# Attention and routed experts on one core: how the two halves of a head's output are added

## The chip, the cores and the metric

The kernel runs on one core of one Trainium2 chip. The metric is the device time of one execution in microseconds (us). A core has TensorE (PE in the profile; its weight loads are listed apart as PEld), VectorE (DVE), ScalarE (ACT), GpSimd (POOL), SyncE (SP, which issues most DMAs) and 16 DMA engines. Each engine takes its instructions in order and waits on semaphores for the others. SBUF is the on-chip memory of 128 partitions; PSUM holds what TensorE writes.

## What is computed

```python
# per batch b (4), head (8): q, k, v are 576 x 64
scores = 0.125 * rotate(q) @ rotate(k).T
attn = softmax(scores)                  # rows of 576
head = attn @ v                         # 576 x 64
x = heads side by side                  # 2304 tokens x 512
logits = x @ w_gate                     # 8 experts
gate = sigmoid(x @ w_local)             # keep the expert of the token before, or take a new one
out = p[e] * (relu(x @ w1[e]) @ w2[e])  # one expert e per token
```

All is float32, and the products are made precise enough for the choice of the expert: operands are split into a high and a low part (type fp32r), and the parts are multiplied apart.

## The kernel before

Two heads of one batch make a pair; there are 16 pairs. The attention goes in 144 steps, nine to a pair: a step g issues the scores of tile g+1 (`mm_s`, L267), the row minimum of it on VectorE (L272), the exponentials of tile g on ScalarE (L289), the transposes of tile g-2 (`tr_main`, L325, L335, L341) whose result is split by ScalarE (high part, L303) and VectorE (low part, L307), and up to five products of attention and values for a pair begun eleven steps ago (`pv_mm`, L361). Eight of the nine steps have five such products, one has none.

The pair's output is made in four units u, each of one half h of the tokens (288 columns) and one head a. The weights of the product are the high and the low part of v side by side (64 + 64 columns), so the 128 x 288 result in PSUM has the share of the high part in 64 partitions and that of the low part in the other 64, and these have to be added. `pv_evac` (L363 to L372) does it: ScalarE copies one half to SBUF at the other half's partitions (`tmp`, 64 x 288, L371), and VectorE adds it to the half that stays in PSUM (`xt`, 64 x 288, L372). The two heads of a pair stand in the two halves of one tile `xt` (128 x 576).

Some steps later `gates` (L417 to L460) turns the pair's output into rows of tokens: for each of five blocks of 128 tokens (the last overlaps the fourth) one float32 product with `xt` as the weights and the constant `wid` as the moving operand (L436, tile `gx`). `wid` is an identity of 128 columns with the 18 columns of the pair's gate weights beside it, so one product of 146 columns gives the rows of both heads and their gate scores. `rows(0, 3)` issues three blocks in the step that has no attention product, `rows(3, 2)` two in the next. VectorE scales the results (L444, L446), and DMAs write the rows to DRAM. A float32 product is two instructions on TensorE, each with a weight load of its own.

The order on TensorE is the order of the program (`MAN0`, `MAN2`). On VectorE, ScalarE, GpSimd and SyncE a scheduler of the framework sets the order from step 12 on, from the dependences and estimates of its own, so a change of one instruction there can move others. In the last part of the attention (about 246 to 302 us) the routing of three batches to the experts (`route`) is woven in, mostly on VectorE; then the experts' products follow (L940, L983) until the end, with the routing of the last batch at their begin.

PSUM tiles of one bank come from `ps_t` (four buffers: transposes, `pv`, `gx`), the score tiles from `ps_s` (two buffers of two banks).

Of the kernel before, what the change touches and what calls it, by code (L numbers as in the profile page):

```python
# [10 lines left out]
F32 = mybir.dt.float32  # L11
F32R = mybir.dt.float32r
BF16 = mybir.dt.bfloat16
# [4 lines left out]
ALU = mybir.AluOpType  # L18
AX = mybir.AxisListType

B, H, S, D = 4, 8, 576, 64
NE, DM, DF = 8, 512, 1024
NP = H // 2
NT = B * S
P = 128
NB = 5
NBLK = B * NB
NG = (B - 1) * NB
# [16 lines left out]
MANUAL = KE  # L45
QK_LAST = 121
SPREAD_LAST = 127

TILE_EARLY = ("ffAffsfxBssgCsshD", "ffAffxfsBsCsgsshD", "fffAffxBssChsgssD", "ffAfffxBsssshsCDg", "ffAfffBsssxsshCgD", "fffxAffsBssgssChD")
TILE = "ffHAgfffxBTssshsCsDL"  # L50
# [5 lines left out]
BIG = 4096.0  # L56
TWO23 = 2.0 ** 23
DX = DM + 1
GATES_AT = {13: 4, 14: 7, 15: 4}

SPLITS = (((1, 2, 3, 4, 5, 7), (0, 6)), ((0, 1, 3, 5, 6, 7), (5, 6)), ((3, 4, 5, 6), (1, 5, 6)), ((1, 3, 4, 7), (1, 3, 4)), ((0, 2, 4, 5, 6), (5, 6)), ((3,), (0, 7)), ((2, 5, 6, 7), (4,)))
# [1 line left out]
ZTHR = -1.5 * 2.0 ** -23  # L63

_COLS = {}
_off = 0
for _n, _w in (
    ("iota128", 128), ("code8", 8), ("p1", 1),
    ("keys", NBLK * NE), ("s0", NBLK), ("pad", NBLK), ("tok64", NBLK),
    ("scan0", 8 * NG + 8), ("tile128", 25),  # L70
):
    _COLS[_n] = (_off, _off + _w)
    _off += _w
# [3 lines left out]
def _constants():  # L77
    c = np.zeros((P, NCONST), np.float32)
    p = np.arange(P)

    def put(name, a):
        lo, hi = _COLS[name]
        if a.dtype == np.int32:
            c.view(np.int32)[:, lo:hi] = a
        else:
            c[:, lo:hi] = a

    put("iota128", np.arange(128)[None])
    put("code8", 7 - np.arange(8)[None])
    put("p1", p[:, None] + 1)  # L90
    tok = np.zeros((P, NBLK))
    tok64 = np.zeros((P, NBLK))
    s0 = np.zeros((P, NBLK))
    pad = np.zeros((P, NBLK))
    s0[0, ::NB] = 1
    pad[:64, 4::NB] = 64
    for b in range(B):
        for j in range(NB):
            lo = b * S + (j * 128 if j < 4 else S - 128)
            tok[:, b * NB + j] = lo + p  # L100
            tok64[:, b * NB + j] = lo // 64
    put("keys", (TWO23 + 8 * tok[:, :, None] + 7 - np.arange(8)).reshape(P, -1))
    put("s0", s0)
    put("pad", pad.astype(np.int32))
    put("tok64", tok64)
    sc = np.ones((8, NG + 1))
    sc[:, 0] = 0
    put("scan0", sc.reshape(1, -1))
    put("tile128", 128 * np.arange(25)[None])
    return c  # L110
# [27 lines left out]
def tile_attention_moe(ctx, tc, qk, v, tabs, turn, consts, tri, wg, wts, out):  # L138
    nc = tc.nc
    pe, act, dve, pool, sp = nc.tensor, nc.scalar, nc.vector, nc.gpsimd, nc.sync  # L140
    outf = out.rearrange("b s d -> (b s) d")

    const = ctx.enter_context(tc.tile_pool(name="const", bufs=1))
    pt_p = ctx.enter_context(tc.tile_pool(name="pt", bufs=4))
    pk_p = ctx.enter_context(tc.tile_pool(name="pk", bufs=4))
    xt_p = ctx.enter_context(tc.tile_pool(name="xt", bufs=XT))
# [7 lines left out]
    ps_t = ctx.enter_context(tc.tile_pool(name="ps_t", bufs=4, space=bass.MemoryType.PSUM))  # L154

    cst = const.tile([P, NCONST], F32, name="cst")
    C = {n: cst[:, a:b] for n, (a, b) in _COLS.items()}
    trib = const.tile([P, P], BF16, name="trib")
    onesb = const.tile([P, P], BF16, name="onesb")

    wid = const.tile([P, 2, 164], F32, name="wid")
    ident = wid[:, 0, 18:146]
    stage = const.tile([P, 7168], F32, name="stage")

    over = ctx.enter_context(tc.tile_pool(name="over", bufs=1))
# [12 lines left out]
    trif = stage[:, 7040:7168]  # L178

    v2_t, m_t, pthi, ptlo, pkhi, pklo, xt_t, sum_t = {}, {}, {}, {}, {}, {}, {}, {}  # L180
    s_t, e_t, tmp_t, pv_t = {}, {}, {}, {}
    qtail0 = None

    NPAIR = B * NP
# [178 lines left out]
    def pv_evac(p, u):  # L363
        h, a = divmod(u, 2)
        if u == 0:
            xt_t[p] = xt_p.tile([P, S], F32, tag="xt", name=f"xt_{p}")
            tmp_t[p] = xt_p.tile([P, S], F32, tag="xt", name=f"tmp_{p}")
        own, other = slice(64 * a, 64 * a + 64), slice(64 - 64 * a, 128 - 64 * a)
        hs = slice(h * HALF, (h + 1) * HALF)
        ps, tmp, xt = pv_t.pop((p, u)), tmp_t[p], xt_t[p]  # L370
        act.copy(tmp[own, hs], ps[other])  # L371
        dve.tensor_tensor(xt[own, hs], ps[own], tmp[own, hs], op=ALU.add)  # L372

    ohr = const.tile([P, NBLK, P], BF16, name="ohr")
    oha = const.tile([P, NBLK, NE], F32, name="oha")
# [41 lines left out]
    def gates(p):  # L417

        b, hp = divmod(p, NP)
        heads = slice(2 * hp, 2 * hp + 2)  # L420
        if hp == 0:
            gm_t[b] = small([P, NB, H, 9], "gm")
        r = sum_t[b].rearrange("p (h j) -> p h j", j=NB)[:, heads]

        def sums():
            act.copy(r[64:128, 1, 4:5], r[64:128, 0, 4:5])
            act.copy(r[64:128, 0, 4:5], r[0:64, 0, 4:5])
            flat = sum_t[b][:, 2 * hp * NB:(2 * hp + 2) * NB]
            act.add(flat, flat, 1e-9)
            dve.reciprocal(flat, flat)  # L430

        def rows(j0, n):
            ps = ps_t.tile([P, n, 146], F32, tag="t", name=f"gx_{p}_{j0}")
            for j in range(j0, j0 + n):
                lo = j * P if j < 4 else S - P
                pe.matmul(ps[:, j - j0], xt_t[p][:, lo:lo + P], wid[:, hp // 2, 18 * (hp % 2):18 * (hp % 2) + 146],  # L436
                          start=True, stop=True)
            rj = r[:, :, j0:j0 + n].rearrange("p a j -> p j a")
            xr = et_p.tile([P, S], F32, tag="et", name=f"xrow_{p}_{j0}")[:, 0:n * P]
            x = xr.rearrange("p (j a d) -> p j a d", a=2, d=D)  # L440
            o, w = ((18, 0), (0, 128))[hp % 2]
            px = ps[:, :, o:o + P].rearrange("p j (a d) -> p j a d", d=D)
            pw = ps[:, :, w:w + 18].rearrange("p j (a e) -> p j a e", e=9)
            dve.tensor_tensor(gm_t[b][:, j0:j0 + n, heads], pw, bc(rj, 3, 9), op=ALU.mult)  # L444
            if j0 == 0 or not ACT_ROWS:
                dve.tensor_tensor(x, px, bc(rj, 3, D), op=ALU.mult)  # L446
            else:
                for j in range(n):
                    for a in range(2):
                        act.activation(x[:, j, a], px[:, j, a], AF.Copy, scale=rj[:, j, a:a + 1])  # L450
            t0 = 1 + b * S
            cols = slice(P * hp, P * hp + P)
            m = min(j0 + n, 4) - j0
            sp.dma_start(rows_d[t0 + j0 * P:t0 + (j0 + m) * P, cols].rearrange("(j p) d -> p j d", p=P),
                         xr.rearrange("p (j d) -> p j d", d=P)[:, 0:m])
            if m < n:

                sp.dma_start(rows_d[t0 + 4 * P:t0 + S, cols], xr[64:128, m * P:n * P])

        return [sums, lambda: rows(0, 3), lambda: rows(3, 2)]  # L460
# [358 lines left out]
    other = []  # L819
# [84 lines left out]
    def gather(t):  # L904
# [6 lines left out]
        else:  # L911
# [3 lines left out]
        pool.indirect_dma_start(  # L915
            out=x[:, 0:DX], out_offset=None, in_=rows_d[0:top + 1],
            in_offset=bass.IndirectOffsetOnAxis(ap=gidx[:, t:t + 1], axis=0),
# [264 lines left out]
    if True:  # L1182
# [40 lines left out]
        for g in range(NSTEP):  # L1223
            if g == GM:
                begin.close()
            with tc.manual_schedule(engines=None if g < GM else MAN0):
                p, i = divmod(g, 9)
                if i == 0 and p % NP == 0:
                    b = p // NP
# [13 lines left out]

                if i == 0 and 2 <= p and p + 2 < NPAIR or g == SPREAD_LAST:
                    spread(p + 1)
# [24 lines left out]
                f = todo.pop(0) if todo else None  # L1270
# [55 lines left out]
def _laid_out(q, k, v, moe_w_gate, moe_w_local, moe_w1, moe_w2):  # L1326
    def turned(x):
        t = x.reshape(B, NP, 2, S, 2, D // 2).transpose(0, 1, 2, 4, 5, 3)
        x = np.stack([t.reshape(B, NP, 2, D, S), t[:, :, :, ::-1].reshape(B, NP, 2, D, S)], axis=4)
        x[:, :, 1] = x[:, :, 1, :, ::-1].copy()  # L1330

        for hp in range(2):
            y = x[0, hp].copy()
            y[1] = x[0, hp, 1, :, ::-1]
            x[0, hp] = y.transpose(2, 1, 0, 3)
        return x.reshape(B, NP, P, 2, S)

    qk = np.concatenate([turned(q), turned(k)], axis=3)
    vp = v.reshape(B, NP, 2, S, D)
    vm = vp[:, :, :, :512].reshape(B, NP, 8, P, D)  # L1340
    vt = np.zeros((B, NP, 2, P, D), np.float32)
    for a in range(2):
        vt[:, :, a, 64 * a:64 * a + 64] = vp[:, :, a, 512:]
    vv = np.concatenate([vm, vt], axis=2).transpose(0, 1, 3, 2, 4)
    w9 = np.concatenate([moe_w_gate, moe_w_local], axis=1).reshape(NP, 2, D, 9)
    wg = np.zeros((2, D, NP, 2, 9), np.float32)
    for a in range(2):
        wg[a, :, :, a] = w9[:, a].transpose(1, 0, 2)
    wg = wg.reshape(P, 2, 2, 18)
    eye = np.broadcast_to(np.eye(P, dtype=np.float32)[:, None], (P, 2, P))  # L1350
    wid = np.concatenate([wg[:, :, 0], eye, wg[:, :, 1]], axis=2)
    w1 = moe_w1.reshape(NE, 4, P, DF).transpose(0, 2, 1, 3).reshape(NE, P, 4 * DF)
    w2 = moe_w2.reshape(NE, 8, P, DM).transpose(0, 2, 1, 3).reshape(NE, P, 8 * DM)
    return {
        "qk": qk, "v": vv, "tabs": _tables(), "turn": _turn(), "consts": _constants(), "tri": _triangle(),
        "wg": wid, "wts": np.concatenate([w1, w2], axis=2),
    }
# [21 lines left out]
```

## Time and profile before

| | us |
|---|---|
| median of 3 runs | 542.3 (542.2 to 542.64) |
| profiled execution | 542.01 |
| its span (first to last instruction) | 540.2 |
| TensorE busy | 517.6 (96%) |
| VectorE busy | 387.3 (72%) |
| ScalarE busy | 345.3 (64%) |
| GpSimd busy | 330.1 (61%) |

The busy shares are means over two unlike parts. In the attention (up to about 302 us) TensorE, VectorE and ScalarE are all busy nearly throughout; in the experts' part TensorE alone is. The busy time of TensorE counts a matmul from its start to a modelled end, and successive ones overlap; the start of one weight load to the start of the next shows better what an instruction costs there. A line of the profile names source line, engine, operation, tiles (out<-in) and shapes.

### The profile page before, as it was taken

The numbers are of one execution on the slowest core, as the hardware profiler recorded it, in microseconds if no ns is written. First come the engines' busy times: TensorE is split into PE (matmuls) and PEld (weight loads), VectorE is DVE, ScalarE is ACT, GpSimd is POOL, SyncE is SP. The second block draws the span as 40 slices with busy tenths as digits, with TensorE's granted clock in tenths as the row PEclk, the third lists the DMA queues.
The fourth block names the chain that finished last, engine by engine and source line by source line (L and its number), as shares of the span: only waits on it lengthen the run. The fifth ranks groups of instructions, "written<-read, shape, count | busy, mean of one in ns | idle before, by whom it ended". The sixth has DMA issues, their size and how long they took to land.

```text
span 540.2 us, 10711 instructions
## 1 busy us (share of the span) xinstructions
PE 517.6 (96%) x3273; PEld 459.2 (85%) x3273; DVE 387.3 (72%) x725; ACT 345.3 (64%) x767; POOL 330.1 (61%) x245
## 2 busy tenths in 40 slices
PE   7989999999999999998999999999999999999993
PEld 4888999999999999997888788887888888888882
DVE  6998999999999999999999935528422736421731
ACT  4988889888999999987676623353533443532440
POOL 4998999888777988986598402337511455411332
PEclk9999999999999999999999999999999999999997
DMA  8659687866887787895288305371637495637350
GB/s 281 273 130 225 199 245 223 205 182 188 226 233 178 214 223 199 206 233 141 38 190 244 85 20 177 123 268 44 231 99 244 125 342 146 217 100 234 82 175 26
DMA packets 63610, 97.37 MB, mean 180 GB/s; under 512 B 28145, under 2 KB 38897, under 8 KB 61746
## 3 DMA queue, kind: packets, MB, share of 16 engines
q1 hardware_dynamic: 60066, 86.48, 56.3%
q0 software_dynamic: 3040, 9.71, 5.6%
q8 instruction: 28, 0.46, 0.3%
q14 instruction: 44, 0.36, 0.2%
q10 hardware_dynamic: 432, 0.36, 0.2%
HBM read 76.98 MB, written 12.86 MB: 166 GB/s over the span
## 4 chain that ended last, share of the span: by engine, by line
PE 63%; DVE 19%; ACT 8%; issue 5%; DMA 2%; POOL 2%; SPq 1%; POOLq 0%; DVEq 0%; ACTq 0%
PE h L940 18%; PE o L983 17%; PE s L267 8%; PE pv L361 8%; DVE mn L272 6%; PE tm L325 6%; DVE ptl L307 4%; ACT e L289 3%; ACT pth L303 2%; PE th L974 2%; PE tx L926 1%; DVE xt L372 1%; DVE pkl L307 1%; PE gx L436 1%; DVE w L885 1%
## 5 line engine op out<-in xcount | busy, mean ns | idle before, releaser
L983 PE MATMUL o<-w,hs 128*128 128x512 f32 x456 | 113.0, 397 | 0.0
L272 DVE TENSOR_REDUCE mn<-s 128x1 f32<-128x576 f32 x144 | 107.4, 746 | 4.1 <-PE s L267 2.7
L940 PE MATMUL h<-w,xs 128*128 128x512 f32 x444 | 106.1, 392 | 0.9 <-DVE xs L307 0.5
L289 ACT ACTIVATE e<-s,mn 128x576 f32<-128x576 f32 x128 | 95.2, 744 | 16.9 <-DVE mn L272 13.6
L267 PE MATMUL s<-m,qst 128*128 128x288 f32 x512 | 97.1, 310 | 6.1 <-ACT e L289 4.0
L307 DVE TENSOR_TENSOR ptl<-tm,pth 128x512 fp32r<-128x512 f32 x139 | 95.0, 684 | 6.5 <-ACT pth L303 3.4
L989 POOL DMA_INDIRECT out_dram<-os,sidx x19 | 23.3, 1227 | 124.0 <-ACTq L891 70.7
L940 PEld LDWEIGHTS h<-w,xs 128*128 128x128 f32 x444 | 82.5, 188 | 19.1 <-DVE w L885 1.1
L983 PEld LDWEIGHTS o<-w,hs 128*128 128x128 f32 x456 | 83.0, 188 | 17.0 <-DVE hs L307 0.4
L303 ACT CAST pth<-tm 128x512 fp32r<-128x512 f32 x139 | 80.9, 582 | 12.4 <-PE tm L325 11.3
L267 PEld LDWEIGHTS s<-m,qst 128*128 128x128 f32 x512 | 74.6, 188 | 12.0 <-ACT e L289 6.6
L325 PE MATMUL tm<-wid,e 128*128 128x128 f32 x512 | 77.0, 272 | 0.9 <-ACT e L289 0.5
L361 PE MATMUL pv<-pth,v 128*128 128x288 f32 x256 | 76.5, 314 | 0.4 <-DVE ptl L307 0.2
L361 PE MATMUL pv<-ptl,v 128*128 128x288 f32 x256 | 76.5, 314 | 0.0
L196 POOL TENSOR_TENSOR stage<-stage 128x1152 f32<-128x1152 f32 x26 | 69.0, 2665 | 8.1 <-DMA stage<-in_qk_dram 6.2
L325 PEld LDWEIGHTS tm<-wid,e 128*128 128x128 f32 x512 | 62.0, 140 | 1.7 <-ACT e L289 0.7
L885 DVE TENSOR_TENSOR w<-stage,w 128x1024 fp32r<-128x1024 f32 x37 | 50.9, 1409 | 15.3 <-DMA stage<-in_wts_dram 7.5
L361 PEld LDWEIGHTS pv<-pth,v 128*128 128x128 f32 x256 | 48.2, 188 | 2.9 <-DVE ptl L307 0.9
L361 PEld LDWEIGHTS pv<-ptl,v 128*128 128x128 f32 x256 | 48.3, 189 | 0.0
L307 DVE TENSOR_TENSOR xs<-tx,xs 128x512 fp32r<-128x512 f32 x19 | 13.1, 689 | 44.0 <-ACTq L891 34.3
L307 DVE TENSOR_TENSOR hs<-th,hs 128x512 fp32r<-128x512 f32 x26 | 17.5, 687 | 30.8 <-ACTq L891 19.1
L197 POOL TENSOR_TENSOR stage<-stage 128x576 f32<-128x576 f32 x26 | 37.0, 1430 | 0.2
(199 smaller groups left out, 814.1 us busy)
## 6 DMA issues: line engine op xcount, KB each, us to landing
stage<-in_wts_dram SPq DMA_DIRECT2D x84, 512.0 KB
stage<-in_qk_dram SPq DMA_DIRECT2D x13, 1152.0 KB
qst<-xq SPq DMA_DIRECT2D x56, 128.0 KB
stage<-in_v_dram SPq DMA_DIRECT2D x16, 320.0 KB
m<-xq SPq DMA_DIRECT2D x14, 288.0 KB
m<-xk SPq DMA_DIRECT2D x14, 288.0 KB
m<-xq SPq DMA_DIRECT2D x14, 256.0 KB
m<-xk SPq DMA_DIRECT2D x14, 256.0 KB
```

The costliest lines, as they stand in the source:

```text
L196: engine.tensor_tensor(x, x, tab[:, 2 * f:2 * f + 2], op=ALU.mult)
L197: engine.tensor_tensor(rr[:, f], x[:, 0], x[:, 1], op=ALU.add)
L267: pe.matmul(st[:, h, lo:hi], lhs, keys[:, k0:k0 + hi - lo], start=(n == 0), stop=(n == len(parts_) - 1))
L272: dve.tensor_reduce(mn, s_t[g][:, :, 0:HALF], axis=AX.XY, op=ALU.min)
L289: act.activation(dst.rearrange("p (h s) -> p h s", h=2), s_t.pop(g)[:, :, 0:HALF], AF.Exp, bias=mn, scale=-1.0, accum_out=sums[:, col:col ...
L303: act.copy(hi, src)
L307: dve.tensor_tensor(lo, src, hi.bitcast(F32), op=ALU.subtract)
L325: pe.transpose(ps[:, k], src[:, k * P:(k + 1) * P], ident)
L361: pe.matmul(pv_t[p, u], lhs.rearrange("p c d -> p (c d)"), rhs, start=(n == 0), stop=(n == 9))
L885: (pool if k in on_pool else dve).tensor_tensor(lo, src, hi.bitcast(F32), op=ALU.subtract)
L940: pe.matmul(ps[:, c], xs_t[t][:, x, k], w[y][:, c * 512:(c + 1) * 512], start=(k == 0 and n == 0), stop=(k == 3 and n == 2))
L983: pe.matmul(ps, hs_t[t][:, x, k], w[y][:, (k % 2) * 512:(k % 2 + 1) * 512], start=(k == 0 and n == 0), stop=(k == 7 and n == 2))
```

## The change

`pv_evac` has no addition any more: ScalarE copies all 128 partitions of the unit's result at once, and the two heads go to two tiles `xt0` and `xt1` (128 x 576 each, in the buffers that `xt` and `tmp` had). The sum is left to the product that turns the rows. For each block of tokens there are now two products, one for each head, each with that head's tile as the weights (128 partitions: high and low share) and 73 columns of the new `wid` as the moving operand: two 64 x 64 identities on top of each other, which add the shares, and beside them, also twice, the head's 9 gate columns. The result in PSUM has 146 columns a block, as before. `wid` grows from 328 to 456 columns; to make room, two constants (`iota128`, `scan0`) are kept in 16 bits, in half the columns, so that `consts` shrinks from 510 to 382 columns. `EVAC_DVE` lists units that VectorE would copy in place of ScalarE; it is empty.

```diff
+EVAC_DVE = ()
+WG = D + 18
+HALVES = ("iota128", "scan0")
...
-    wid = const.tile([P, 2, 164], F32, name="wid")
-    ident = wid[:, 0, 18:146]
+    wid = const.tile([P, P + NP * WG], F32, name="wid")
+    ident = wid[:, 0:P]
...
     def pv_evac(p, u):
         h, a = divmod(u, 2)
         if u == 0:
-            xt_t[p] = xt_p.tile([P, S], F32, tag="xt", name=f"xt_{p}")
-            tmp_t[p] = xt_p.tile([P, S], F32, tag="xt", name=f"tmp_{p}")
-        own, other = slice(64 * a, 64 * a + 64), slice(64 - 64 * a, 128 - 64 * a)
+            xt_t[p] = [xt_p.tile([P, S], F32, tag="xt", name=f"xt{a}_{p}") for a in range(2)]
         hs = slice(h * HALF, (h + 1) * HALF)
-        ps, tmp, xt = pv_t.pop((p, u)), tmp_t[p], xt_t[p]
-        act.copy(tmp[own, hs], ps[other])
-        dve.tensor_tensor(xt[own, hs], ps[own], tmp[own, hs], op=ALU.add)
+        ps, xt = pv_t.pop((p, u)), xt_t[p][a]
+        if u in EVAC_DVE:
+            dve.tensor_copy(xt[:, hs], ps)
+        else:
+            act.copy(xt[:, hs], ps)
...
-            ps = ps_t.tile([P, n, 146], F32, tag="t", name=f"gx_{p}_{j0}")
+            ps = ps_t.tile([P, n, 2 * WG], F32, tag="t", name=f"gx_{p}_{j0}")
             for j in range(j0, j0 + n):
                 lo = j * P if j < 4 else S - P
-                pe.matmul(ps[:, j - j0], xt_t[p][:, lo:lo + P], wid[:, hp // 2, 18 * (hp % 2):18 * (hp % 2) + 146],
-                          start=True, stop=True)
+                for a in range(2):
+                    w0 = P + hp * WG + (9 if a == 0 else 0)
+                    pe.matmul(ps[:, j - j0, a * (D + 9):(a + 1) * (D + 9)], xt_t[p][a][:, lo:lo + P], wid[:, w0:w0 + D + 9],
+                              start=True, stop=True)
...
-            o, w = ((18, 0), (0, 128))[hp % 2]
-            px = ps[:, :, o:o + P].rearrange("p j (a d) -> p j a d", d=D)
-            pw = ps[:, :, w:w + 18].rearrange("p j (a e) -> p j a e", e=9)
+            px = ps.rearrange("p j (a d) -> p j a d", a=2)[:, :, :, 0:D]
+            pw = ps[:, :, D:WG].rearrange("p j (a e) -> p j a e", e=9)
```

On TensorE the products that turn the rows become twice as many, at the same places. The program of the kernel before, with the products of pair 2 (`gx`) in the step of pair 5 that has no attention product, and the two blocks of the next step:

```order
L325 MATMUL tm_1558<-wid,e_2_1468 128x128 x4
L436 MATMUL gx_0_1565<-wid,xt_1134 128x146 x3
L267 MATMUL s_1578<-m_1312,qst_100 128x288 x4
L325 MATMUL tm_1585<-wid,e_3_1525 128x128 x4
L361 MATMUL pv_3_1592<-pth_1087,v_3_850 128x288
```

And the same place of the changed kernel:

```order
L330 MATMUL tm_1553<-wid,e_2_1465 128x128 x4
L443 MATMUL gx_0_1560<-wid,xt_2_1131 128x73
L443 MATMUL gx_0_1560<-wid,xt_2_1132 128x73
L443 MATMUL gx_0_1560<-wid,xt_2_1131 128x73
L443 MATMUL gx_0_1560<-wid,xt_2_1132 128x73
L443 MATMUL gx_0_1560<-wid,xt_2_1131 128x73
L443 MATMUL gx_0_1560<-wid,xt_2_1132 128x73
L272 MATMUL s_1576<-m_1309,qst_100 128x288 x4
L330 MATMUL tm_1583<-wid,e_3_1521 128x128 x4
L366 MATMUL pv_3_1590<-pth_1084,v_3_845 128x288
```

Three products of 146 columns have become six of 73; nothing else moved. On ScalarE the scheduler's order at the same place is another one. Before (`pth<-tm_1585` is the split of the transposes that stand behind `gx` on TensorE, `et` the exponentials of the pair's last tile):

```order
L303 CAST pth_1378<-tm_1527 128x4x128
L371 COPY tmp_1426<-pv_2_1509 64x288
L289 ACTIVATE e_3_1525,sum_1286<-s_1520,mn_1548 128x576
L303 CAST pth_1378<-tm_1558 128x4x128
L429 ACTIVATE sum_1286<-sum_1286 128x10
L303 CAST pth_1378<-tm_1585 128x4x128
L289 ACTIVATE et_1583,sum_1286<-s_1550,mn_1576 128x576
```

And of the changed kernel (there that split is `pth<-tm_1583`):

```order
L308 CAST pth_1376<-tm_1523 128x4x128
L294 ACTIVATE e_3_1521,sum_1283<-s_1516,mn_1543 128x576
L377 COPY xt_3_1423<-pv_2_1505 128x288
L434 ACTIVATE sum_1283<-sum_1283 128x10
L308 CAST pth_1376<-tm_1553 128x4x128
L294 ACTIVATE et_1581,sum_1283<-s_1545,mn_1574 128x576
L308 CAST pth_1376<-tm_1583 128x4x128
```

The exponentials `et` stood behind the split that waits for the transposes after `gx`, and now stand ahead of it. The order before that is shown is the one at the begin of pairs 3 to 7; from pair 8 on the kernel before, too, has `et` first, and the changed kernel has it first in all of these.

## Rows read from the trace of the kernel before

**Rows 1.** Page, part 4: shares of the chain that ended last.
```profile
PE 63%; DVE 19%; ACT 8%; issue 5%; DMA 2%; POOL 2%; SPq 1%; POOLq 0%; DVEq 0%; ACTq 0%
```

**Rows 2.** Stretches: start:end and length; per engine busy us (instructions); clock, DMA share, GB/s.
```profile
11.20:62.90 51.70, 47.85 (x345) 44.18 (x346) 47.44 (x90) 45.79 (x122) 47.98 (x30) 1.00 0.73 219
62.90:146.40 83.50, 82.29 (x636) 79.97 (x635) 78.78 (x153) 74.53 (x191) 71.47 (x49) 1.00 0.78 212
146.40:228.50 82.10, 82.10 (x647) 80.83 (x646) 79.64 (x157) 75.85 (x190) 70.22 (x47) 1.00 0.78 203
228.50:246.10 17.60, 17.49 (x138) 17.02 (x137) 16.92 (x35) 15.40 (x40) 15.41 (x12) 1.00 0.87 239
246.10:287.80 41.70, 37.94 (x290) 33.96 (x289) 40.45 (x96) 29.15 (x71) 30.81 (x38) 1.00 0.58 134
287.80:302.00 14.20, 13.45 (x90) 12.13 (x89) 13.00 (x30) 11.09 (x22) 10.84 (x8) 1.00 0.61 170
```

**Rows 3.** The same stretches, instructions on tile xt alone (PE, PEld, DVE).
```profile
11.20:62.90 51.70, 0.91 (x6) 0.90 (x7) 3.14 (x7) 1.00 0.73 219
62.90:146.40 83.50, 7.84 (x50) 6.72 (x50) 9.01 (x20) 1.00 0.78 212
146.40:228.50 82.10, 7.84 (x50) 6.83 (x50) 9.03 (x20) 1.00 0.78 203
228.50:246.10 17.60, 2.23 (x15) 1.95 (x14) 1.81 (x4) 1.00 0.87 239
246.10:287.80 41.70, 3.21 (x20) 2.73 (x20) 3.58 (x8) 1.00 0.58 134
287.80:302.00 14.20, 3.24 (x20) 2.70 (x20) 2.28 (x5) 1.00 0.61 170
```

**Rows 4.** Groups by shape: count | busy us, mean ns | idle before, releasers.
```profile
L372 DVE TENSOR_TENSOR xt<-pv,tmp 64x288 f32<-64x288 f32 x64 | 28.8, 451 | 1.8 <-ACT tmp L371 0.4 <-issue 0.3
...
L436 PE MATMUL gx<-wid,xt 128*128 128x146 f32 x160 | 25.3, 289 | 0.0
L371 ACT COPY tmp<-pv 64x288 f32<-64x288 f32 x64 | 25.3, 395 | 4.5 <-PE pv L361 2.8
...
L436 PEld LDWEIGHTS gx<-wid,xt 128*128 128x128 f32 x160 | 21.8, 189 | 0.3 <-DVE xt L372 0.3
...
L1111 ACT CAST m<-k 128x288 fp32r<-128x288 f32 x6 | 2.4, 409 | 0.6 <-PE k L1103 0.5
```

**Rows 5.** Weight loads around one rows(0, 3): start, us, line, count.
```profile
211.09 0.80 PEld L436 LDWEIGHTS gx<-wid,xt 128*128 128x128 f32 x6
211.82 0.31 PEld L267 LDWEIGHTS s<-m,qst 128*128 128x128 f32 x2
```

**Rows 6.** Weight loads behind the two instructions of a float32 product of 64 columns.
```profile
18.73 0.19 PEld L1103 LDWEIGHTS k<-raw,turn 128*128 128x128 f32 x1
18.84 0.19 PEld L267 LDWEIGHTS s<-m,qst 128*128 128x128 f32 x1
```

**Rows 7.** Waits from 62.9 to 146.4 us: us, times, longest.
```profile
PEld s L267 <- ACT et L289: 2.3, 5, 0.5
```

**Rows 8.** Waits from 146.4 to 228.5 us.
```profile
PEld pv L361 <- DVE ptl L307: 0.5, 3, 0.2
```

**Rows 9.** ScalarE behind rows(0, 3), one pair: start, us, line, idle before.
```profile
96.36 0.59 ACT L303 CAST pth<-tm 128x512 fp32r<-128x512 f32 x1 [1.02 <-PE tm L325]
96.85 0.75 ACT L289 ACTIVATE et<-s,mn 128x576 f32<-128x576 f32 x1
```

**Rows 10.** VectorE: an addition and what follows it.
```profile
204.30 0.45 DVE L372 TENSOR_TENSOR xt<-pv,tmp 64x288 f32<-64x288 f32 x1
204.68 0.74 DVE L272 TENSOR_REDUCE mn<-s 128x1 f32<-128x576 f32 x1
```

**Rows 11.** Waits from 246.1 to 287.8 us.
```profile
ACT e L289 <- DVE mn L272: 6.4, 6, 1.9
```

**Rows 12.** The last pair's rows: weight loads.
```profile
297.57 0.80 PEld L436 LDWEIGHTS gx<-wid,xt 128*128 128x128 f32 x6 [0.26 <-DVE xt L372]
```

More of the change, by code (lines that the diff above doesn't have):

```diff
@@ L65 @@
 _COLS = {}
+HALVES = ("iota128", "scan0")
 _off = 0
 for _n, _w in (
-    ("iota128", 128), ("code8", 8), ("p1", 1),
+    ("iota128", 64), ("code8", 8), ("p1", 1),
     ("keys", NBLK * NE), ("s0", NBLK), ("pad", NBLK), ("tok64", NBLK),
-    ("scan0", 8 * NG + 8), ("tile128", 25),
+    ("scan0", 4 * NG + 4), ("tile128", 25),
 ):
@@ L84, in put @@
             c.view(np.int32)[:, lo:hi] = a
+        elif name in HALVES:
+            c.view(np.uint16)[:, 2 * lo:2 * hi] = a.astype(np.float32).view(np.uint32) >> 16
         else:
@@ L156, in tile_attention_moe @@
     cst = const.tile([P, NCONST], F32, name="cst")
-    C = {n: cst[:, a:b] for n, (a, b) in _COLS.items()}
+    C = {n: cst[:, a:b].bitcast(BF16) if n in HALVES else cst[:, a:b] for n, (a, b) in _COLS.items()}
     trib = const.tile([P, P], BF16, name="trib")
     onesb = const.tile([P, P], BF16, name="onesb")
-    wid = const.tile([P, 2, 164], F32, name="wid")
-    ident = wid[:, 0, 18:146]
+    wid = const.tile([P, P + NP * WG], F32, name="wid")
+    ident = wid[:, 0:P]
     stage = const.tile([P, 7168], F32, name="stage")
@@ L180, in tile_attention_moe @@
     v2_t, m_t, pthi, ptlo, pkhi, pklo, xt_t, sum_t = {}, {}, {}, {}, {}, {}, {}, {}
-    s_t, e_t, tmp_t, pv_t = {}, {}, {}, {}
+    s_t, e_t, pv_t = {}, {}, {}
     qtail0 = None
@@ L1345, in _laid_out @@
     w9 = np.concatenate([moe_w_gate, moe_w_local], axis=1).reshape(NP, 2, D, 9)
[L1346 to L1351, printed above, removed]
+    eye = np.eye(P, dtype=np.float32)
+    one = [np.concatenate([w[1], eye[:D, :D], w[0]], axis=1) for w in w9]
+    wid = np.concatenate([eye, np.tile(np.concatenate(one, axis=1), (2, 1))], axis=1)
     w1 = moe_w1.reshape(NE, 4, P, DF).transpose(0, 2, 1, 3).reshape(NE, P, 4 * DF)
```

## Prediction, on record before the changed kernel was run

> **What bounds the kernel now.** I read the chain that ended last first, then the busy times by stretches, then the waits of the stretches, then single places. The chain is 63% TensorE and 19% VectorE [rows 1], so the change touches both engines that matter: it takes work from the second and gives work to the first. A mean over the span doesn't say which of the two counts where, so I cut the attention at the pairs' starts. From 146.4 to 228.5 us (pairs 8 to 12) TensorE is busy 82.10 of 82.10 us, and even its weight loads, which leave out the tails of the matmuls, 80.83 [rows 2]. From 62.9 to 146.4 us (pairs 3 to 7) it is 82.29 of 83.50, the loads 79.97. VectorE has 79.64 and 78.78 there, ScalarE 75.85 and 74.53: three engines are nearly full, but the one with nothing left is TensorE. From 246.1 to 287.8 us this turns: VectorE is busy 40.45 of 41.70 us, the loads of TensorE only 33.96, ScalarE 29.15 [rows 2]. That is where the routing stands in VectorE's queue, and ScalarE's exponentials wait 6.4 us for its minima [rows 11]. So VectorE's time is worth something in 42 us of the attention, and TensorE's in some 165.
>
> **What is taken away.** 64 additions of 451 ns [rows 4]. VectorE starts the next instruction before the old one has ended: 204.30 to 204.68 is 0.38 us for one [rows 10], which is the price that I use. They are spread over the attention, 20 in each of the two full stretches, 8 in the stretch that VectorE bounds [rows 3]. The copies on ScalarE stay 64 in number and 288 columns long; they have 128 partitions now. The 64-partition copy takes 395 ns, a 128-partition conversion of the same length 409 [rows 4]: at most 64 x 0.014 = 0.9 us on an engine that doesn't bound, taken as nothing.
>
> **What is added.** 160 matmul instructions become 320 (two to each float32 product), half as wide, each with its own load of 128 x 128 weights. Six of them at present take 211.09 to 211.82 us, 0.73 us or 0.122 us each, from load to load [rows 5]. For the new ones the trace has one near relative, a float32 product of 64 columns: behind its two instructions the loads start at 18.73 and 18.84 us, 0.11 us apart [rows 6]. If the stream of columns were the limit, an instruction of 73 columns would take half of 0.122, 0.061 us. So with few columns the loading of the weights sets the pace, and halving the columns saves nearly nothing. Bounds: 0.061 us (columns alone; the additional loads then cost nothing), and 0.189 us, the whole duration of a load [rows 4], if loads did not overlap at all. I take 0.11, the row that is nearly the same instruction. An old instruction then becomes 2 x 0.11 - 0.122 = 0.098 us longer; a pair has ten: 1 us a pair, 15.7 us in all. The other ends make it 0 and 160 x 0.256 = 41 us.
>
> The Trainium skill states both rules: "TensorE: Matmul & The Clock Gate", section "LDWEIGHTS (loading the stationary operand)", gives a load as its columns over 1.2 GHz, some 107 ns for 128 whatever the moving side is, and the section "Back-to-back issue gap" gives an isolated matmul as columns over 2.4 GHz and 2.5 ns, an estimate of 63 ns for two passes of 73. By the first the change costs what I take from the rows, by the second it costs nothing. The rows at 64 columns agree with the first; the second becomes a rival below.
>
> **Stretch by stretch.**
> 62.9 to 228.5 us, pairs 3 to 12: 100 old instructions [rows 3] x 0.098 = +9.8 us, on an engine with no room. Two things come back. In pairs 3 to 7 TensorE waits five times, 2.3 us in all, for the exponentials `et` [rows 7]: ScalarE has the split of the transposes behind `gx` ahead of them, sits idle 1.02 us for it and starts `et` only at 96.85 [rows 9]. In the new order of ScalarE `et` stands first, as it does in pairs 8 to 12, where this wait doesn't occur: -2.3. And the 0.5 us in which the attention products wait for VectorE's low parts [rows 8] go: -0.5. The sum is +7.0. The 40 additions that VectorE loses here are worth nothing beyond that: they were beside a full TensorE.
> 228.5 to 246.1 us: 15 instructions, +1.5; the loads leave 0.58 us idle [rows 2] that a lighter VectorE can fill: +0.9.
> 246.1 to 287.8 us: VectorE bounds; 8 additions x 0.38 = -3.0. The 20 instructions of `gx` (+2.0) go into 7.7 us in which TensorE loads nothing. Bounds -3.6 (8 x 0.451) and +2.0 (if TensorE's delays at `gx` are passed on).
> 287.8 to 302 us, the last pairs: 20 instructions, +2.0. The last pair's product waits 0.26 us for the addition [rows 12], which is gone. Five additions leave VectorE, which is busy 13.00 of 14.20, and some of TensorE's idle time (14.20 - 12.13) covers the rest: I take +1.0, between -1.9 and +2.0.
> 11.2 to 62.9 us: no engine is full (47 to 48 of 51.7). Seven additions could give 2.7, six or seven instructions cost 0.6: I take -0.5.
> Moved DMAs: none but the two constants, 64 KB more and 64 KB less; at the 219 GB/s of the second stretch [rows 2] that is 0.3 us before the first transposes at worst, taken as 0. The 16-bit constants are read only in the routing, with columns and partitions unchanged: 0.
> After 302 us nothing changes; the experts' products, on TensorE, shift with their begin.
> The sum: 7.0 + 0.9 - 3.0 + 1.0 - 0.5 = +5.4 us. The profiled execution took 542.01 us (span 540.2 and 1.8 around it), 0.3 under the median of the runs; by the profile the changed kernel takes 547.4, against the runs 547.7. That is the forecast.
>
> **Rivals.**
> A, the other side: the columns set the pace, not the loads. Then `gx` costs what it did, and the relief alone is left: -2.8 in pairs 3 to 12 (waits of rows 7 and 8), -0.6, -3.0, and -0.5 and -1.0 at the two ends: 534.4 us. It decides if the new instructions stand under about 0.075 us apart, where 100 x (2 x 0.075 - 0.122) equals the 2.8. For it: the old instructions are paced by their columns, at 0.122 us each [rows 5] above the 0.11 us between loads. Against it: rows 6, the one place with so few columns.
> B, the additional loads hide in idle time: the loads leave 3.5 and 1.3 us idle in the two full stretches [rows 2], and a VectorE with 10% less to do may let TensorE use all of it: 9.8 - 4.8 = +5.0, then +0.9, -3.6, 0 and -2.1: +0.2, 542.5 us. Against it: TensorE's order is fixed, and it waits on ScalarE as much as on VectorE.
> C, the bursts hurt: the products of one step now hold TensorE for 1.3 us where they held it for 0.73; ScalarE idles meanwhile, and lacks that time after, since it is busy 90% itself. Then nothing comes back: 9.8 + 1.5 + 2.0 + 0.6 and -1.0 in VectorE's stretch: +12.9, 555 us. For it: the 1.02 us idle of rows 9; against it: with `et` first ScalarE has work in hand for that time.
>
> **How the numbers follow.** The forecast 0.64, with 544.5 to 550.5 of its own (VectorE's stretch and the last pairs move it by 3 either way); A 0.10, B 0.16, C 0.10. The range 541.5 to 551.5 takes in the forecast and most of B and leaves out A and most of C. A measurement of this kernel can tell about 0.2%, 1.1 us, from no change. Faster by more: A and a quarter of B, 0.14. Within: about half of B, 0.10. Slower: 0.76.
>
> **What would show it.** Right: the loads of `gx` stand 0.11 us apart, twelve in 1.3 us; pairs 8 to 12 take about 17.3 us instead of 16.4, with TensorE as full as before; VectorE falls from 97% busy there to some 82% ((79.64 - 9.03) of 86.5 us); the wait of `s` for `et` is gone in pairs 3 to 7; from the start of pair 14 to the last exponentials it takes some 3 us less. Wrong: loads 0.06 us apart (A), pairs at 16.8 with no idle time of TensorE (B), or new waits of TensorE for ScalarE behind `gx` (C).

## The result and the profile after

The changed kernel takes 549.15 us (median of 4 runs, 548.37 to 549.73), the kernel before 542.25 beside it: a ratio of 1.0125, with a 95% interval of 1.0107 to 1.0142. The change costs about 7 us; 547.7 was forecast. The profiled execution of the changed kernel took 549.64, its span is 547.9. Line numbers have grown by five or six (L372's copy is L377, `gx` L443, the minimum L277).

The chain that ended last (page, part 4) answers to [rows 1]: VectorE's 19% have become 8, ScalarE's 8 have become 1, and TensorE's 63 have become 85.

```profile
PE 85%; DVE 8%; issue 3%; POOL 2%; ACT 1%; DMA 0%; POOLq 0%; SPq 0%; DVEq 0%
```

The stretches, cut as in [rows 2]: the edges between the lines are the starts of ScalarE's first exponentials of pairs 3, 8, 13 and 14 and of its last ones, so the lengths of the four lines between them can be compared with those of before. Columns as in [rows 2] (TensorE, its loads, VectorE, ScalarE, GpSimd; clock, DMA share, GB/s):

```profile
11.40:60.50 49.10, 45.85 (x333) 42.51 (x334) 43.60 (x80) 44.35 (x122) 44.24 (x29) 1.00 0.73 221
60.50:146.40 85.90, 85.90 (x697) 85.55 (x697) 74.66 (x136) 73.39 (x192) 74.24 (x50) 1.00 0.80 212
146.40:232.20 85.80, 85.80 (x697) 85.45 (x697) 74.64 (x136) 72.95 (x192) 69.75 (x47) 1.00 0.77 193
232.20:254.10 21.90, 20.75 (x167) 20.23 (x166) 17.65 (x33) 14.81 (x41) 18.02 (x14) 1.00 0.73 192
254.10:293.40 39.30, 36.08 (x273) 34.55 (x274) 37.04 (x85) 27.06 (x68) 28.06 (x35) 0.96 0.53 131
293.40:308.00 14.60, 14.60 (x128) 14.26 (x127) 9.91 (x24) 10.61 (x24) 9.67 (x7) 1.00 0.66 190
```

Pairs 3 to 7 take 85.90 us where they took 83.50, pairs 8 to 12 85.80 for 82.10, pair 13 21.90 for 17.60, pairs 14 and 15 up to the last exponentials 39.30 for 41.70. In the second and third stretch TensorE's loads leave 0.35 us idle in 86, where [rows 2] leave 3.5 and 1.3: it is now full by any measure, and a pair takes 17.17 us throughout. VectorE has fallen from 97% to 87% there. The fifth line holds two things that were not forecast: VectorE still has 37.04 of 39.30, and the granted clock is 0.96.

The groups by shape that answer to [rows 4] (count, busy us, mean ns, idle before):

```profile
L443 PE MATMUL gx<-wid,xt 128*128 128x73 f32 x320 | 39.4, 271 | 0.4 <-DVE ptl L312 0.4
L443 PEld LDWEIGHTS gx<-wid,xt 128*128 128x128 f32 x320 | 38.5, 191 | 0.6 <-DVE ptl L312 0.6
...
L377 ACT COPY xt<-pv 128x288 f32<-128x288 f32 x64 | 25.6, 400 | 3.5 <-PE pv L366 3.3
```

The 128-partition copy takes 400 ns, 5 more than that of 64 partitions: free, as taken. A load lasts what it lasted; what one costs is read from the timeline, which answers to [rows 5]:

```profile
197.08 1.42 PEld L443 LDWEIGHTS gx<-wid,xt 128*128 128x128 f32 x12
198.42 0.57 PEld L272 LDWEIGHTS s<-m,qst 128*128 128x128 f32 x4
```

Twelve loads hold TensorE from 197.08 to 198.42: 1.34 us, 0.112 each. Six old ones held it for 0.73.

Where the 7.6 us of span came in, between equal events of the traces (the starts of those exponentials, and of the experts' first product). "Forecast" is the prediction's term for the difference between before and after; the four columns at the right are experiments told below:

| us | before | after | forecast | loads alone | relief alone | after, scores on VectorE | relief, scores on VectorE |
|---|---|---|---|---|---|---|---|
| start to pair 3 | 62.94 | 60.50 | -0.5 | 61.50 | 59.90 | 59.64 | 60.99 |
| pairs 3 to 7 | 83.43 | 85.88 | +2.6 | 87.23 | 80.92 | 85.86 | 80.93 |
| pairs 8 to 12 | 82.15 | 85.82 | +4.4 | 87.03 | 81.01 | 85.85 | 81.01 |
| pair 13 | 17.55 | 21.85 | +0.9 | 19.55 | 20.92 | 19.46 | 17.69 |
| pairs 14 and 15, to the last exponentials | 41.74 | 39.40 | -3.0 | 40.06 | 37.49 | 38.65 | 37.78 |
| to the experts | 10.51 | 12.93 | +1.0 | 11.73 | 12.44 | 12.92 | 12.45 |
| to the end | 241.91 | 241.49 | 0 | 242.16 | 242.89 | 241.92 | 243.60 |

Pairs 3 to 12 lose 6.1 us, and the late attention (the start of pair 13 to the experts) takes 74.18 us for 69.80: it loses 4.4, where it was to gain 1.1. Pair 13 alone loses 4.3. There the waits from 232.2 to 254.1 (us, times, longest) have a new one:

```profile
ACT ex L500 <- DVE d L497: 2.4, 1, 2.4
DVE mx L494 <- POOL lg_all L474: 1.5, 1, 1.5
```

`mx` is the first instruction of the routing on VectorE; it reads the gate scores `lg_all`, which GpSimd sums for this batch. VectorE's timeline around it (start, us, instruction, idle before):

```profile
248.79 0.76 DVE L277 TENSOR_REDUCE mn<-s 128x1 f32<-128x576 f32 x1
251.09 0.28 DVE L494 TENSOR_REDUCE mx<-lg_all 128x15 f32<-128x120 f32 x1 [1.55 <-POOL lg_all L474]
251.29 0.68 DVE L312 TENSOR_TENSOR ptl<-tm,pth 128x512 fp32r<-128x512 f32 x1
251.89 1.46 DVE L497 TENSOR_TENSOR d<-lg_all,mx 128x120 f32<-128x120 f32 x1
253.26 0.74 DVE L277 TENSOR_REDUCE mn<-s 128x1 f32<-128x576 f32 x1
```

From one minimum to the next 4.47 us go by: VectorE waits 1.55 us for GpSimd, and then `d` lasts 1.46. TensorE shows the consequence:

```profile
252.52 0.29 PE L366 MATMUL pv<-ptl,v 128*128 128x288 f32 x1
252.66 0.29 PE L366 MATMUL pv<-pth,v 128*128 128x288 f32 x1
254.94 0.80 PE L272 MATMUL s<-m,qst 128*128 128x288 f32 x4 [1.99 <-ACT et L294]
...
257.01 0.44 PE L366 MATMUL pv<-ptl,v 128*128 128x288 f32 x1
257.25 0.44 PE L366 MATMUL pv<-pkh,v 128*128 128x288 f32 x1
...
259.69 0.30 PE L366 MATMUL pv<-ptl,v 128*128 128x288 f32 x1
259.82 0.29 PE L366 MATMUL pv<-pth,v 128*128 128x288 f32 x1
```

It stands idle for 1.99 us, behind exponentials that waited for that minimum. A second loss follows: products that stand 0.13 us apart at 259.7 stand 0.24 apart at 257. The stretches behind the wait say why:

```profile
254.94:255.90 0.96, 0.96 (x7) 0.96 (x8) 0.96 (x4) 0.42 (x1) 0.00 (x0) 1.00 0.32 68
255.90:259.30 3.40, 3.40 (x17) 3.38 (x16) 2.41 (x9) 2.70 (x7) 1.90 (x3) 0.50 0.92 210
259.30:261.00 1.70, 1.70 (x16) 1.70 (x15) 1.10 (x3) 1.31 (x3) 1.70 (x2) 0.99 0.96 237
```

About a microsecond after TensorE had resumed, its granted clock fell to 0.50, 1.2 GHz in place of 2.4, for 3.4 us. The busy columns don't show it: TensorE reads as 100% busy, at half the speed.

### The profile page after: what moved, and what is told of

It is laid out like the page before. It is cut to its first block, busy times and chain, and to the rows that moved or that the text cites. A ratio compares the mean times of both kernels' runs of the same rounds, so it can differ in the third digit from the quotient of the medians.

```text
span 547.9 us, 10966 instructions
## 1 busy us (share of the span) xinstructions
PE 528.5 (96%) x3433; PEld 475.7 (87%) x3433; DVE 369.4 (67%) x661; ACT 337.8 (62%) x767; POOL 327.3 (60%) x245
## 4 chain that ended last, share of the span: by engine, by line
PE 85%; DVE 8%; issue 3%; POOL 2%; ACT 1%; DMA 0%; POOLq 0%; SPq 0%; DVEq 0%
PE h L946 19%; PE o L989 16%; PE pv L366 14%; PE s L272 13%; PE tm L330 10%; PE gx L443 6%; DVE mn L277 2%; PE th L980 2%; DVE ptl L312 2%; PE tx L932 1%; PE tk L340 1%; PE wake_ps L1101 1%; POOL w L890 1%; POOL out_dram L995 1%; DVE qst L1149 1%
## 5 line engine op out<-in xcount | busy, mean ns | idle before, releaser
L277 DVE TENSOR_REDUCE mn<-s 128x1 f32<-128x576 f32 x144 | 108.1, 750 | 5.5 <-PE s L272 3.7
L272 PE MATMUL s<-m,qst 128*128 128x288 f32 x512 | 94.2, 307 | 5.2 <-ACT e L294 2.6
L989 PEld LDWEIGHTS o<-w,hs 128*128 128x128 f32 x456 | 83.0, 188 | 17.4 <-DVE hs L971 0.4
L443 PE MATMUL gx<-wid,xt 128*128 128x73 f32 x320 | 39.4, 271 | 0.4 <-DVE ptl L312 0.4
L443 PEld LDWEIGHTS gx<-wid,xt 128*128 128x128 f32 x320 | 38.5, 191 | 0.6 <-DVE ptl L312 0.6
```

The lines of the kernel that those rows point to most:

```text
L272: pe.matmul(st[:, h, lo:hi], lhs, keys[:, k0:k0 + hi - lo], start=(n == 0), stop=(n == len(parts_) - 1))
L277: dve.tensor_reduce(mn, s_t[g][:, :, 0:HALF], axis=AX.XY, op=ALU.min)
L443: pe.matmul(ps[:, j - j0, a * (D + 9):(a + 1) * (D + 9)], xt_t[p][a][:, lo:lo + P], wid[:, w0:w0 + D + 9], start=True, stop=True)
L989: pe.matmul(ps, hs_t[t][:, x, k], w[y][:, (k % 2) * 512:(k % 2 + 1) * 512], start=(k == 0 and n == 0), stop=(k == 7 and n == 2))
```

## The experiments

The ratios are to the kernel before on the same chip (542.48 and 542.46 us there, medians of 11 and 17 runs).

**Loads alone.** The kernel before, with each product of `gx` in two halves of 73 columns; the additions stay on VectorE.

```diff
-                pe.matmul(ps[:, j - j0], xt_t[p][:, lo:lo + P], wid[:, hp // 2, 18 * (hp % 2):18 * (hp % 2) + 146],
-                          start=True, stop=True)
+                for a in range(2):
+                    w0 = 18 * (hp % 2) + 73 * a
+                    pe.matmul(ps[:, j - j0, 73 * a:73 * a + 73], xt_t[p][:, lo:lo + P], wid[:, hp // 2, w0:w0 + 73],
+                              start=True, stop=True)
```

> The kernel before, with its additions on VectorE kept, and each product of 146 columns that turns the rows made as two of 73 columns (same weights, same result). Theory (the loading of the weights sets the pace, 0.11 us an instruction): loads of gx 0.11 us apart, pairs 8 to 12 about 17.3 us instead of 16.4, and without the relief on VectorE more is lost than in the changed kernel: about 553 us, 550 to 556. Rival (the columns set the pace; the changed kernel lost its time elsewhere): 542 to 543 us, pairs 8 to 12 unchanged.

Measured: 550.39 us, ratio 1.0142 (1.0125 to 1.0159); pairs of 17.4 us. Twelve loads of `gx` take the same 1.34 us, and TensorE is full, while VectorE has 81.16 us to do in five pairs (two rows of loads, and the five pairs up to the fourth step of pair 12):

```profile
199.94 1.42 PEld L438 LDWEIGHTS gx<-wid,xt 128*128 128x128 f32 x12
201.28 0.57 PEld L267 LDWEIGHTS s<-m,qst 128*128 128x128 f32 x4
```

```profile
139.24:226.29 87.05, 87.05 (x696) 85.77 (x696) 81.16 (x159) 75.44 (x191) 66.11 (x46) 1.00 0.78 205
```

So the loss is that of the loads, and without the relief it is larger: 8.7 us in pairs 3 to 12, where the changed kernel loses 6.1. In the late attention the same loads cost 1.5 us; they fill idle time there, and what TensorE's loads leave idle falls from 9.7 to 5.4 us.

**Relief alone.** The kernel before without the additions: ScalarE copies one half, which leaves out the share of the low part of v; the products of `gx` stay 146 columns wide.

```diff
-        act.copy(tmp[own, hs], ps[other])
-        dve.tensor_tensor(xt[own, hs], ps[own], tmp[own, hs], op=ALU.add)
...
+        act.copy(xt[own, hs], ps[0:64])
```

> The kernel before, with its products of 146 columns kept, and the share of the low part of v left out of the output: ScalarE copies the high half straight to xt (64 x 288, as before), and VectorE adds nothing. So it has the relief of VectorE without the additional loads. Theory (TensorE is full in pairs 3 to 13; the relief takes the waits of 2.8 us there, and 3 us where VectorE bounds): 534 to 540 us, likeliest 537, pairs 8 to 12 unchanged at 16.3 to 16.4 us. Rival (VectorE paces the attention): over 15 us faster, pairs 8 to 12 below 16 us. Rival (the scheduler puts the routing's first step ahead, as in the changed kernel, and eats the gain of the late stretch): 539 to 541 us.

Measured: 537.84 us, ratio 0.9915 (0.9897 to 0.9933). A pair takes 16.20 us from pair 4 to pair 13; two stretches, of four and of five pairs, up to the fourth step of pair 12:

```profile
66.83:131.63 64.80, 64.80 (x519) 64.52 (x518) 58.18 (x110) 59.91 (x153) 57.89 (x41) 1.00 0.83 222
131.63:212.63 81.00, 81.00 (x648) 80.65 (x647) 72.79 (x137) 74.97 (x191) 70.04 (x48) 1.00 0.83 219
```

From the start of pair 3 to that of pair 13 the relief gives 3.7 us, where the named waits are 2.8: not only those went, nearly all idle time of the loads did (0.7 us are left of 4.8). In the late attention it gave nothing and lost 1.0 (70.85 for 69.80): here too `mx` stands ahead and waits, 2.5 us, for GpSimd, TensorE pauses for 1.98 us, and its clock is at 0.50 from about 244.0 to 247.5. The total came out as expected, but in part by luck: 3.0 us came ahead of pair 3, which the expectation did not name, and from pair 13 on nothing was left of the 3 us that it had put there.

**The changed kernel with the third batch's scores on VectorE.** If the wait of `mx` for GpSimd is what the late attention loses by, a reduction on VectorE itself takes it away.

```diff
-        if b < B - 1:
+        if b < B - 2:
...
-            dve.tensor_reduce(lg_all[:, 0:NB], g.rearrange("p j h e -> p j e h"), axis=AX.X, op=ALU.add)
+            j0 = b * NB if b < B - 1 else 0
+            dve.tensor_reduce(lg_all[:, j0:j0 + NB], g.rearrange("p j h e -> p j e h"), axis=AX.X, op=ALU.add)
```

> The changed kernel, with the sum of the gate scores of the third batch taken from GpSimd and made by one reduction on VectorE, so that the routing's first instruction there no longer waits for GpSimd. Theory (that wait, 1.5 us, is what turned the expected gain of the late stretch into a loss): 546.5 to 548 us, from the minimum of pair 13 to that of pair 15 some 1.5 to 2.5 us less than in the changed kernel. Rival (the wait only covered other waits, or the order in that stretch costs as much elsewhere): 549 to 550 us.

Measured: 546.15 us, ratio 1.0078 (1.006 to 1.0095). VectorE's timeline at the same place:

```profile
247.82 0.83 DVE L477 TENSOR_REDUCE lg_all<-gm 128x45 f32<-128x360 f32 x1
248.56 0.76 DVE L277 TENSOR_REDUCE mn<-s 128x1 f32<-128x576 f32 x1
...
249.85 0.76 DVE L277 TENSOR_REDUCE mn<-s 128x1 f32<-128x576 f32 x1
250.53 0.27 DVE L495 TENSOR_REDUCE mx<-lg_all 128x15 f32<-128x120 f32 x1
...
251.63 0.27 DVE L498 TENSOR_TENSOR d<-lg_all,mx 128x120 f32<-128x120 f32 x1
252.13 0.75 DVE L277 TENSOR_REDUCE mn<-s 128x1 f32<-128x576 f32 x1
```

`mx` waits no more, `d` takes 0.27 us, the clock stays at 1.00, and the late attention takes 71.03 us for 74.18, although VectorE has 0.83 us more to do. Pairs 3 to 12 are as they were (171.71 for 171.70). The gain is somewhat larger than was expected. The scheduler has also put `mx` back behind the next minimum, where it stood before the change, so the run tells what its early place and its wait cost together.

**Relief alone with the scores on VectorE.** The same edit on the kernel without the additions (it leaves out the same share).

> The kernel before with the share of v's low part left out and no additions on VectorE (as in the run with the relief alone), and the third batch's gate scores summed on VectorE instead of GpSimd. Theory (the early place of the routing's first instruction, which waits for GpSimd, costs some 3 us whether or not the loads are doubled): 534 to 535.5 us, the late stretch 2.5 to 3.5 us shorter than with the relief alone. Rival (that wait matters only where TensorE is late because of the additional loads): 537 to 538.5 us.

Measured: 535.5 us, ratio 0.9872 (0.9854 to 0.989), 2.3 us less than the relief alone. The late attention takes 67.92 us, 2.9 less than with the relief alone and 1.9 less than before: the wait stood in the way of the relief there, with or without the added loads. The kernel before was not run with its scores on VectorE, so it is open how much of the 1.9 that edit would give by itself.

**Wider products.** The changed kernel with 82 columns in place of 73 (nine unused ones beside each head's).

```diff
-                    w0 = P + hp * WG + (9 if a == 0 else 0)
-                    pe.matmul(ps[:, j - j0, a * (D + 9):(a + 1) * (D + 9)], xt_t[p][a][:, lo:lo + P], wid[:, w0:w0 + D + 9],
+                    w0 = P + hp * WG
+                    pe.matmul(ps[:, j - j0, a * WG:(a + 1) * WG], xt_t[p][a][:, lo:lo + P], wid[:, w0:w0 + WG],
...
```

> The changed kernel, with all 82 columns of a pair's block of the constant as the moving operand of each product instead of 73 (the gate columns of the other head are made and not read; the result is the same). Theory (the load of the weights sets the pace, and columns ride free up to it): loads of gx 0.112 us apart as in the changed kernel, pairs 17.2 us. Rival (columns set the pace): a ninth more, 0.125 us apart, pairs 0.2 to 0.3 us longer, about 3 us in all.

Measured: 548.01 us in one run; pairs of 17.18 us. Twelve loads of `gx`, and the place of the long wait of TensorE:

```profile
196.61 1.42 PEld L443 LDWEIGHTS gx<-wid,xt 128*128 128x128 f32 x12
```

```profile
254.62 0.80 PE L272 MATMUL s<-m,qst 128*128 128x288 f32 x4 [2.06 <-ACT et L294]
```

```profile
239.59:259.70 20.11, 18.05 (x143) 17.45 (x142) 16.51 (x36) 14.29 (x38) 15.71 (x16) 1.00 0.61 142
```

The next load starts at 197.95, so one takes 0.112 us as with 73 columns. An eighth more columns cost nothing: the loads set the pace. The run also tells the clock apart from the wait. TensorE stands idle as long as before (2.06 us), but the clock stays at 1.00, and the stretch from the minimum of pair 13's fourth step to that of pair 14's takes 20.11 us, where the changed kernel takes 21.24 and the one with the scores on VectorE 18.08. So by these three traces the low clock is 1.1 us of the loss there, and the wait with the long `d` 2.0. (From the minimum of pair 15's fourth step to the experts it took a microsecond less, too, than the changed kernel; one run doesn't settle why.) The runs of the changed kernel spread in the same way: 549.64 and 549.73 us at mean clocks of 0.992 and 0.991, 548.37 and 548.67 at 0.994.

**Additions on GpSimd in the late pairs.** Can the relief be had without the loads? The kernel before, where ScalarE copies both halves and GpSimd adds them, in pairs 13 and 14; then in pair 13 alone (`p == 13`).

```diff
-        dve.tensor_tensor(xt[own, hs], ps[own], tmp[own, hs], op=ALU.add)
+        if p in (13, 14):
+            act.copy(xt[own, hs], ps[own])
+            pool.tensor_tensor(xt[own, hs], xt[own, hs], tmp[own, hs], op=ALU.add)
+        else:
+            dve.tensor_tensor(xt[own, hs], ps[own], tmp[own, hs], op=ALU.add)
```

> The kernel before, but in pairs 13 and 14, whose output falls in the stretch that VectorE bounds, ScalarE copies both halves of a unit (two copies of 64 x 288) and GpSimd adds them in SBUF; TensorE's work is as before. Theory (8 additions of 0.38 us leave an engine that bounds there, and ScalarE and GpSimd have room): 538.5 to 541 us, the late stretch 1.5 to 3 us shorter. Rival (GpSimd's additions come late or hold VectorE up, or the new order costs what is saved): 542 to 545 us.

> The kernel before, with the additions of pair 13 alone on GpSimd (ScalarE copies both halves for it), since with pairs 13 and 14 on GpSimd the stretch of pair 13's output was 1.1 us shorter by the minimum of pair 15, but the last pairs 3 us longer. Theory (the gain lies where VectorE bounds, and the loss came from GpSimd being late for pair 14 and the experts' weights): 540.5 to 541.8 us. Rival (GpSimd's additions delay what GpSimd does after them): 542 to 545 us.

Measured: 548.43 us, ratio 1.0117 (1.0098 to 1.0135), and 546.21, ratio 1.0072 (1.0058 to 1.0086). Both are misses, by more than either rival allowed for. With both pairs, 1.3 us were gained up to the fourth step of pair 15 (273.96 for 275.30), but then TensorE waits for GpSimd's split of transposes, `ptl`, and at the end of that wait the clock falls (TensorE's wait, and the stretch around its end):

```profile
277.14 0.61 PE L361 MATMUL pv<-ptl,v 128*128 128x288 f32 x1 [1.65 <-POOL ptl L300]
```

```profile
276.90:280.80 3.90, 3.65 (x17) 3.64 (x18) 2.50 (x5) 1.10 (x3) 3.82 (x6) 0.56 0.90 354
```

With pair 13 alone the same wait stands there, 1.65 us, and the clock is 0.55 from 277.0 to 280.8. Why GpSimd is late there, by the additions themselves or by the new order of its queue, was not taken apart.

**Another order on ScalarE.** The kernel before, with ScalarE in the order of the program in steps 12 to 71, to see whether the wait of [rows 7] can be had back by order alone.

```diff
-            with tc.manual_schedule(engines=None if g < GM else MAN0):
+            with tc.manual_schedule(engines=None if g < GM else MAN0 | {mybir.EngineType.Activation} if g < 72 else MAN0):
```

> The kernel before, with ScalarE's order from step 12 to step 71 that of the program and not the scheduler's, so that the exponentials of a step stand ahead of the splits of that step's transposes, those behind the rows' products among them. Theory (in pairs 3 to 7 that order alone costs 0.5 us or more a pair, which the runs without additions show gone): 538.5 to 541 us, pairs 3 to 7 at 16.4 to 16.6 us in place of 17.0. Rival (the program's order makes other waits on ScalarE): 543 us or more.

Measured: 542.66 us, ratio 1.0012 (1.0 to 1.0023): no gain, and pairs 3 to 7 still take 17.0 us each. The wait for `et` has shrunk from 2.3 us to 0.5, but from 68.6 to 153.4 us others stand in its place:

```profile
ACT e L289 <- DVE mn L272: 4.2, 9, 0.9
...
PEld s L267 <- ACT e L289: 2.9, 7, 0.8
```

In the order of the program the 2.3 us of [rows 7] only change their name. What `et` put ahead by itself would give stays open, since this run moved everything else on ScalarE too.

No kernel with all of the computation beat the kernel before.

## Why the prediction was right or wrong, point by point

**The price of the added products: right.** 0.112 us per instruction were measured for 0.11 taken, at 73 columns and at 82. On top of the relief the loads of pairs 3 to 12 cost 171.70 - 161.93 = 9.8 us; the sum had +9.8. The Trainium skill, "TensorE: Matmul & The Clock Gate", section "LDWEIGHTS (loading the stationary operand)", counts a load by its columns, an estimate of 107 ns; the spacing of the loads in the trace agrees, with 112 ns, while a load taken by itself lasts 191. Rival A, with instructions under 0.075 us apart, is out.

**What comes back in pairs 3 to 12: somewhat too small.** The prediction said that the lost additions are worth nothing beyond the waits of [rows 7] and [rows 8], -2.8. The relief alone gave -3.7, and the sum came to +6.1 there in place of +7.0: in pairs 3 to 7 it was +2.4 for +2.6, in pairs 8 to 12 +3.7 for +4.4. Loads and relief draw on the same idle time: loads alone cost 174.26 - 165.58 = 8.7, since they fill some of it themselves, and the relief on top of them gives back 2.6. The named waits were the ones the trace could put a releaser to; the loads' idle time in [rows 2], 4.8 us, was a bound that held, and rival B had taken it. But B itself is out: the loads cost twice what idle time there was, and a pair takes 17.17 us, not 16.8.

**Ahead of pair 3: too small.** -2.4 was measured for -0.5 taken. It came in pair 2, 15.55 us from its first exponentials to those of pair 3, where the kernel before takes 18.00. The relief alone has 15.76 there, but the loads alone have 16.50, so it isn't the relief only; what it is was not taken apart.

**The order of ScalarE: the wait went, and why is open.** In pairs 3 to 7 no wait of `s` for `et` is left, and `et` stands ahead of the split, which itself still waits 0.99 us behind `gx`:

```profile
94.86 0.75 ACT L294 ACTIVATE et<-s,mn 128x576 f32<-128x576 f32 x1
...
96.69 0.59 ACT L308 CAST pth<-tm 128x512 fp32r<-128x512 f32 x1 [0.99 <-PE tm L330]
```

With loads alone and with relief alone `et` stands ahead as well, and the wait is gone in both, with the additions and without. The order of the program, in the last experiment, put `et` ahead too and gained nothing: TensorE then waited for other exponentials, which waited for VectorE's minima. In pairs 3 to 12 the changed kernel has no wait of TensorE for ScalarE, in spite of ScalarE's idle time behind `gx`, so rival C is out too.

**The late attention: the step that failed.** +0.9 - 3.0 + 1.0 = -1.1 was forecast, +4.3 - 2.3 + 2.4 = +4.4 measured. "VectorE bounds; 8 additions x 0.38 = -3.0", and the 0.58 us of idle time ahead of it that a lighter VectorE can fill, supposed that VectorE's order stays as it is. The scheduler put `mx` a step earlier into the room, ahead of scores that GpSimd had not summed yet. The early place with its wait, `d` held up behind it, and the low clock after TensorE's pause cost 74.18 - 71.03 = 3.2 us, by the run without them. (Not all of this need be new: the kernel before has a hold-up like that of `d`, told in the last section.) The sign that was named, some 3 us less from the start of pair 14 to the last exponentials, came nearly true, 39.40 for 41.74 (38.65 with the scores on VectorE): the price of the additions held, and the loss stands mostly ahead of that edge, where `mx` and its wait had moved.

What is left of the late attention, 71.03 for 69.80, is the relief (-1.9, 67.92 for 69.80) against the loads (+3.1, 71.03 for 67.92), which alone had cost 1.5. On top of the relief the loads fill less idle time: what TensorE's loads leave idle falls from 7.6 to 4.9 us there, with loads alone from 9.7 to 5.4. Why is open. The last part, from the last exponentials to the experts, came to +2.4 where +1.0 was taken and +2.0 was the bound; the relief alone has +1.9 there, the loads alone +1.2. And in pair 15, at 283.98, TensorE waits for GpSimd, a wait (here from 280.95 to 306.38) that neither the kernel before nor the loads alone have:

```profile
PE pv L366 <- POOL ptl L305: 1.3, 1, 1.3
```

**The end, and VectorE's share.** After the attention -0.4 was measured for nothing taken. VectorE's share in pairs 8 to 12 was told as some 82% and is 87%: the prediction took off whole durations, 20 of 0.45 us, though it had itself read 0.38 for one, and busy time fell by 5.0. In five pairs the durations added up fall from 87.6 to 79.4 us, about as told, but VectorE now waits 8.7 us ahead of `ptl` (1.1 before), and its instructions overlap less, by 4.8 us in place of 7.8. (The 219 GB/s in the sum of the DMAs are those of the first line of [rows 2], not the second; nothing hangs on it.)

The total is near because errors offset: -2.4 ahead of pair 3 where -0.5 stood and +6.1 in pairs 3 to 12 where +7.0 stood, against +4.4 from pair 13 on where -1.1 stood. That 547.7 lies so near 549.15 is in part luck.

## What to carry to other kernels

Splitting a float32 product by columns doubles its loads; at 73 and 82 columns the load of 128 columns sets the pace, 0.112 us an instruction, where one of 146 columns takes 0.122, so half the columns save nearly nothing. Where two engines are both near full, the idle time of the bounding one is a common pot: price relief and load against it once, not each by its named waits. An engine that gets lighter lets a scheduler move instructions forward; before crediting it, look in the new order for what now stands ahead of critical work and waits for a third engine.

## What the runs showed of the hardware that was not expected

Behind a pause of TensorE the clock could fall, and did not always. In the traces of the changed kernel (a pause of 1.99 us), of the relief alone (1.98) and of both kernels with additions on GpSimd (1.65) it fell to 0.50, at the end of the pause or up to 1 us after it, for about 3.4 us. Behind other pauses as long it stayed at 1.00: 2.06 us in the kernel with 82 columns, 2.07 and 2.06 at 272.74 and 270.91 us in the two runs with the relief alone, 1.60 at 287.01 with pair 13's additions on GpSimd. So a wait of 2 us could cost another 1.1 us, and not in every run.

VectorE's `d` (128 x 120) lasts 1.46 us in the changed kernel and 0.27 with the scores on VectorE. In the first case GpSimd had begun a long instruction over SBUF just ahead, and both end within 0.2 us of each other:

```profile
251.78 1.41 POOL L212 TENSOR_TENSOR xq<-stage,xq 128x576 fp32r<-128x576 f32 x1
```

The kernel before has the same at another instruction with two inputs, `rs`, which takes 0.17 us in the changed kernel:

```profile
247.00 1.38 DVE L501 SCALAR_TENSOR_TENSOR rs<-lg_all,cst 128x15 f32<-128x15 f32 x1
```

There `xq` had begun at 246.93, for 1.42 us. With loads alone `d` starts 0.92 us after `xq` and lasts 0.65. In each of the ten traces the first of `d` and `rs` to meet `xq` ends within 0.2 us of its end, while `mx` and `ptl`, where they stand beside it, take no longer than elsewhere (0.28 with the relief and the scores on VectorE, 0.69 with loads alone).

The Trainium skill, "SBUF — State Buffer", section "SBUF: two separate sides", under "Who interferes with whom", has a rule that fits: a VectorE instruction with two inputs in SBUF and a GpSimd instruction that reads SBUF take a port in turn, for the whole of an instruction; by it `d` and `rs` waited for `xq`. The traces agree, though no run here was made to vary it by itself.
